# Attention and gated MLP on one core: z2 stores, maxima and sums on other queues, heads packed in pairs, refills by credit

## The chip, the cores and the metric

The kernel runs on one core of a Trainium2 chip, in float32. Its time is the device time of one execution in microseconds (us); the smaller the better. Every number of a profile is from one execution recorded by the hardware profiler.

## The reference

A sequence of 2048 rows of 576 is normalised once; attention and a gated MLP both read it, and the result is their product, gated, added to the input.

```python
xn = layernorm(x)
# attention: 32 heads of 18, a causal window of 256 keys
qkv = (xn @ wqkv).reshape(B, S, 3, 32, 18)
scores = einsum("bhqd,bhkd->bhqk", q, k) * 18 ** -0.5
mask = (q_row - k_row >= 0) & (q_row - k_row < 256)
s = softmax(where(mask, scores, -1e9)) @ v -> (B, S, 576) @ wo
# gated MLP
z = gelu(xn @ w_in)                       # 576 -> 4608
z1, z2 = z[..., :2304], layernorm(z[..., 2304:])
g = einsum("ts,bsf->btf", w_sp, z2) + b_sp   # mixes the 2048 rows
out = x + s * silu((z1 * g) @ w_out)
```

## The kernel before

Matrix products are made exact enough by splitting each operand into a rounded high part (ScalarE copies) and a low part (VectorE subtracts), and by three products of the parts. The program runs through six stages:

- **Start, Q and K** (0 to 176 us). Rows are normalised and transposed into `xt6`, Q and K come out transposed, and each strip is stored to `st_d` in DRAM: for Q and for K (first index), high and low parts of 18 rows each, by head. `load_wqkv` splits the weights; the low part is made by GpSimd (L259).
- **V** (to 208 us).
- **z2** (208 to 460 us): 6 x 16 steps of 14 matmuls (L686). ScalarE applies GELU into `zt` (L697), VectorE takes statistics, and two steps at a time are stored to `z2_d` by a DMA on ScalarE's queue (L700). Beside it GpSimd forms sums and differences of w_sp (`sp_combos`, L619 to L623), which SyncE loads (`a<-in_w_sp`) and stores (`sc_d<-a`). Six head loads and the first 42 steps of row maxima are put in too.
- **Attention with z1** (460 to 992 us): 16 units of four heads and half of the queries. A unit computes scores transposed (`tps`, L524), exponentials on ScalarE (`pt`, L528), causal masks on GpSimd (L531, L534) and the product with V (`ops`, L547), four steps later. Between these matmuls stand those of z1 (L445) and the maxima for the next unit.
- **Spatial mixing** (992 to 1716 us): w_sp @ z2 by seven products of blocks (a Strassen scheme), 168 steps of 18 matmuls (L960); each step needs a piece of w_sp and a piece of z2, which `z_unit` loads (`zr`) and forms. `pump` hands out these units.
- **Output** (1716 us to the end).

Row maxima: for unit u, `row_max` computes scores the other way round (`sp`, L395), a maximum per query on VectorE (L399), one transposition for all 32 maxima, and splits the negated maxima into two parts. `put_max` writes them by DMA on ScalarE's queue (L415) into rows 54 and 55 of the head's Q strip; there K has ones, so that the matmul itself subtracts the maximum. RMN is the number of steps of a unit, LEAD how many are done ahead of their unit.

A head lies in half of a slot (`att`, five slots of two heads): partitions 0 to 55 for even heads, 64 to 119 for odd ones. `load_head` fills it by four DMAs of SyncE (L362 to L365), of 36, 18, 20 and 36 partitions. Slots 3 and 4 are made and cleared where attention starts. LOAD_AT gives the items of a unit (32 or 40) ahead of which the loads of later heads stand.

When a unit's last block is out, `finish` gathers the softmax sums by a DMA on ScalarE's queue (`den<-ou`, L597); VectorE inverts them, SyncE stores them (`r_d`, L573) and reads them back, each head's over 32 partitions (`rp`, L577, 512 KB); VectorE multiplies, SyncE stores four strips (`o_d`, L588).

In the start the order of each engine's work comes from a scheduler; from z2 on it is the order in which the code writes it, for all five engines. Each engine waits in that order, and what stands behind a wait waits too. SyncE issues nearly all DMAs; a DMA that waits for its data holds up those behind it.

Of the kernel before, what the change touches and what calls it, by code (L numbers as in the profile page):

```python
# [62 lines left out]
def kernel(  # L63
# [20 lines left out]

    st_d = dram.tile([2, 38, H, S], F32, name="st_d")
    sc_d = dram.tile([4, 8, P, 1024], F32, name="sc_d")
# [21 lines left out]
    low = const.tile([64, 1], F32, name="low")  # L108
    dve.reduce_sum(low, ident[:64, :64].rearrange("p (a n b) -> p n a b", n=2, b=8)[:, 1], axis=mybir.AxisListType.XY)
    dve.tensor_scalar(low, low, -1.0, None, ALU.mult)  # L110
# [118 lines left out]
    with ExitStack() as early:  # L229
# [15 lines left out]
        with ExitStack() as ph:  # L245
# [7 lines left out]
            def load_wqkv(c):  # L253
                raw = pA.tile([P, 5, 192], F32, name="wraw", bufs=4)
                sp.dma_start(raw, wqkv[:, :, c * 192:(c + 1) * 192])
                to, c = (wq, c) if c < 6 else (wv, c - 6)
                cs = slice(c * 192, (c + 1) * 192)
                act.activation(to[0][:, :, cs], raw, AF.Copy)
                pool.tensor_tensor(to[1][:, :, cs], raw, f32(to[0][:, :, cs]), ALU.subtract)  # L259

# [39 lines left out]
            def qk_chunk(c):  # L300
                cs = slice(c * 512, (c + 1) * 512)
                for n, j in enumerate(range(9) if c < NC - 1 else (0, 4, 5, 1, 2, 3, 6, 7, 8)):
                    if n == NORM_AT and c + 1 < NC:
                        norm_chunk(c + 1)
                    js = slice(j * P, (j + 1) * P)
                    ps = mmp.tile([P, 512], F32, name="mm")
                    pl = list(passes(whq[:, :, js], wlq[:, :, js], cs))
                    for n, (w, r) in enumerate(pl):
                        pe.matmul(ps, w, r, start=n == 0, stop=n == len(pl) - 1)  # L309
                    hl = pA.tile([P, 2, 512], F32R, name="qkhl")  # L310
                    split(hl[:, 1], hl[:, 0], ps)
                    for n in range(2):
                        rows = st_d[n, 0:36, :, cs].rearrange("(c i) h s -> c i h s", c=2)[:, 2 * j:2 * j + 2]
                        sp.dma_start(rows.rearrange("c i h s -> (i h) c s"), f32(hl[64 * n:64 * n + 64]))
# [8 lines left out]
            for c in range(NC):  # L323
                if c + 1 < NC:
                    load_x(c + 1)
                qk_chunk(c)
                if c == 0:
                    for w in range(6, 9):
                        load_wqkv(w)
                    zero = pA.tile([H, 512], F32, name="zero", bufs=1)  # L330
                    pool.memset(zero, 0.0)
                    for k in range(NC):
                        for r in range(2):
                            sp.dma_start(st_d[0, 36 + r, :, k * 512:(k + 1) * 512], zero)
        aa = open_pool(early, "aa", bufs=2)
        slots = [aa.tile([P, SLOT], F32R, name=f"att{i}", bufs=1) for i in range(3)]

        with ExitStack() as ph:
# [17 lines left out]
            def load_head(u, j):  # L356
                g, half = UNITS[u]
                q0 = half * HS
                k0, kn = (0, HS) if half == 0 else (HS - 256, HS + 256)
                h, b = 4 * g + j, 64 * (j % 2)  # L360
# [23 lines left out]
            def row_max(u):  # L384
                g, half = UNITS[u]
                base = 0 if half == 0 else 6
                mx = aa.tile([P, 4, 2, 8], F32, name="mx")
                for j in range(4):
                    for i in range(8):
# [10 lines left out]
                                                 scalar=-3.0e38, op0=ALU.add, op1=ALU.max,  # L400
                                                 accum_out=mx[:, j, 0, i:i + 1])
# [4 lines left out]
                pe.transpose(pt[:64, :P], mx.rearrange("p a n b -> p (a n b)"), ident)  # L406
                spend(110)
# [100 lines left out]
            def scores(u, kb, qa, qz, j):  # L508
# [3 lines left out]
                if j == 0:  # L512
                    own = u == NU - 1 or len(seen) % NPT < 3
                    pts[u, kb] = ap_.tile([P, 4, 384], F32, name="pt", bufs=3) if own else ab.tile(
                        [P, 4, 384], F32, name="pt2", bufs=NPT - 3)
                    seen.append(u)
# [48 lines left out]
            def finish(u, ou):  # L565
# [30 lines left out]

                act.dma_start(den, ou[DH::32, :])  # L597
                after(6000 if u < NU - 2 else 2700, lambda: queue([invert]))
# [33 lines left out]
            with ExitStack() as gate:  # L632
# [35 lines left out]
                combos = sp_combos(gate)  # L668
                heads_at = {3 * NS + 4 * n: divmod(n, 4) for n in range(6)}
                stream = (step for u in range(NU) for step in row_max(u))  # L670
                for pc in range(6):
# [4 lines left out]
                    if pc == 1:  # L676
                        clear(0)
                        clear(1)
                    for s in range(NS):
                        ss = slice(s * P, (s + 1) * P)  # L680
# [11 lines left out]
                        if pc + 1 < 6 and s % 2 == 0:  # L692
                            next(nxt[2], None)
                        if s % 2 == 0:
                            zz = gz.tile([P, 2 * ZW], F32, name="zt", bufs=4)
                        zv = zz[:, s % 2 * ZW:s % 2 * ZW + ZW]
                        act.activation(zv, ps[:, :ZW], AF.Gelu_apprx_tanh)  # L697
# [9 lines left out]
                        if pc == 5:  # L707
                            dve.bn_aggr(mv2[:, s, :], st2[:, s].rearrange("p a b -> p (a b)"))
                for _ in combos:
                    pass  # L710
# [6 lines left out]
            with ExitStack() as heads:  # L717
                order.close()
                heads.enter_context(tc.manual_schedule(engines=HEADS))
                ab = open_pool(spare, "ab", side="right")  # L720
                for i in range(3, NSLOT):
                    slots.append(ab.tile([P, SLOT], F32R, name=f"att{i}", bufs=1))
                    clear(i)
                work = heads.enter_context(ExitStack())
# [109 lines left out]
    with ExitStack() as ph:  # L834
# [115 lines left out]
        for m, (g, n, s) in enumerate(order_sp):  # L950
# [22 lines left out]
            if s == 5:  # L973
                if g + 1 < NG:
                    units += [z_unit(wk, g + 1, k, b) for b in range(8)]
                elif n:
                    units += free_tile(n)
        while due or units or flying:
            now += 1
            for job in due.pop(now, ()):  # L980
                job()
            pump(1)

# [146 lines left out]
```

## Time and profile before

| what | before |
|---|---|
| median of 3 runs | 1982.95 us (1979.98 to 1985.52) |
| the profiled execution, its span | 1988.46 us, 1986.8 us |
| TensorE busy | 1926.1 us, 97% |
| VectorE, ScalarE, GpSimd busy | 1077.4, 890.8, 286.6 us |
| moved by DMA | 375.05 MB, mean 189 GB/s |
| DMA issues on SyncE's queue, on ScalarE's | 343.62 MB, 29.47 MB |

Busy is the time in which an engine works on something; the space between is idle, and the profile names what ended it. A wait counts only where the engine that sets the end waits, which here is TensorE in nearly all of the span. DMA share is a mean over 16 DMA engines.

### The profile page before, as it was taken

What the parts mean: (1) busy time and instruction counts of PE and PEld (TensorE: products, weight loads), DVE (VectorE), ACT (ScalarE), POOL (GpSimd) and SP (SyncE); (2) the same over time, 40 slices, a digit from 0 to 9 for tenths busy, and PEclk for the clock granted to TensorE, in tenths of its full rate; (3) what the DMA queues carried; (4) which work ended last, traced back from release to release, by engine and by line L of the source; (5) the groups of instructions that cost most, each with busy time, mean ns of one, the idle gap of its engine ahead of it and who ended that gap; (6) DMA issues with size and microseconds to landing.
All of it is one profiled execution on the core that took longest, in us unless ns stands there. A gap on an engine that the chain in (4) does not pass through costs nothing.

```text
span 1986.8 us, 30617 instructions
## 1 busy us (share of the span) xinstructions
PE 1926.1 (97%) x11096; PEld 1661.5 (84%) x11096; DVE 1077.4 (54%) x2286; ACT 890.8 (45%) x1647; POOL 286.6 (14%) x360
## 2 busy tenths in 40 slices
PE   6999999999999999999999999999999999999998
PEld 5889999997777777777688887888788888999998
DVE  6521233256666666666267768576866676523222
ACT  3222222215656656656575465645554445422121
POOL 5000363402222223333200000000000000000000
PEclk9999999999999999999999999999999999999999
DMA  7655798924454656464577578666775567844441
GB/s 221 178 145 146 248 302 265 300 92 126 134 154 135 162 137 161 128 157 115 171 264 240 174 261 271 214 211 217 237 247 182 180 219 247 293 138 141 141 143 56
DMA packets 218599, 375.05 MB, mean 189 GB/s; under 512 B 42960, under 2 KB 115536, under 8 KB 218320
## 3 DMA queue, kind: packets, MB, share of 16 engines
q1 hardware_dynamic: 197520, 343.62, 56.4%
q10 hardware_dynamic: 20928, 29.47, 4.1%
q8 instruction: 87, 1.43, 0.3%
q14 instruction: 64, 0.52, 0.1%
HBM read 259.92 MB, written 112.30 MB: 187 GB/s over the span
## 4 chain that ended last, share of the span: by engine, by line
PE 81%; DMA 11%; DVE 3%; ACT 1%; SPq 1%; issue 1%; POOL 1%; ACTq 0%; DVEq 0%; POOLq 0%
PE acc L960 32%; PE po L1057 12%; PE mm L445 10%; PE mm L686 5%; PE mm L309 5%; PE tps L524 4%; PE sp L395 4%; PE ops L547 3%; PE vps L463 3%; DMA sc_d<-a 3%; DMA att<-st_d 3%; PE wops L1027 2%; DMA a<-in_w_sp_dram 1%; DMA z1raw<-in_w_z_dram 1%; DMA att<-mhl 1%
## 5 line engine op out<-in xcount | busy, mean ns | idle before, releaser
L960 PE MATMUL acc<-sph,zh 128*128 128x512 f32 x1008 | 394.3, 391 | 8.2 <-DVE cb L914 8.2
L960 PE MATMUL acc<-spl,zh 128*128 128x512 f32 x1008 | 393.8, 391 | 0.0
L960 PE MATMUL acc<-sph,zl 128*128 128x512 f32 x1008 | 393.6, 390 | 0.0
L399 DVE CUSTOM_DVE_ANT_0 junk<-sp,band 128x384 bf16<-128x384 f32 (+1 forms) x512 | 272.7, 538 | 152.3 <-PE sp L395 148.1
L528 ACT ACTIVATE pt<-tps 128x384 f32<-128x384 f32 (+2 forms) x576 | 244.6, 438 | 144.7 <-PE tps L524 112.9
L445 PE MATMUL mm<-b,z1wh 128*128 128x512 f32 x648 | 250.7, 398 | 0.0
L213 DVE TENSOR_TENSOR spl<-spr,sph 128x1024 fp32r<-128x1024 f32 x166 | 203.1, 1224 | 62.9 <-ACT sph L213 61.7
L960 PEld LDWEIGHTS acc<-sph,zh 128*128 128x128 f32 x1008 | 190.2, 189 | 48.6 <-ACT zh L213 5.6
L960 PEld LDWEIGHTS acc<-sph,zl 128*128 128x128 f32 x1008 | 190.2, 189 | 40.0
L960 PEld LDWEIGHTS acc<-spl,zh 128*128 128x128 f32 x1008 | 190.3, 189 | 39.5
L524 PE MATMUL tps<-att 128*128 128x384 f32 (+1 forms) x576 | 189.6, 329 | 14.9 <-ACT pt L528 12.0
L686 PE MATMUL mm<-z2wh,b 128*128 128x384 f32 x720 | 194.3, 337 | 7.5 <-ACT zt L697 7.5
L213 ACT ACTIVATE zh<-b 128x384 fp32r<-128x384 f32 x144 | 75.8, 526 | 251.7 <-PE acc L960 251.6
L213 ACT ACTIVATE sph<-spr 128x1024 fp32r<-128x1024 f32 x166 | 174.2, 1049 | 21.5 <-DMA spr<-in_w_sp_dram 11.2
L395 PE MATMUL sp<-att 128*128 128x384 f32 (+1 forms) x512 | 171.3, 335 | 5.6 <-DMA att<-st_d 2.2
L1057 PE MATMUL po<-b,yh 128*128 128x288 f32 x896 | 155.6, 296 | 0.0
L213 DVE TENSOR_TENSOR zl<-b,zh 128x384 fp32r<-128x384 f32 x144 | 79.9, 555 | 124.2 <-ACT zh L213 124.2
L524 PEld LDWEIGHTS tps<-att 128*128 128x128 f32 x576 | 108.8, 189 | 41.7 <-ACT pt L528 25.0
L445 PE MATMUL mm<-b,z1wl 128*128 128x512 f32 x360 | 143.4, 398 | 0.0
L445 PEld LDWEIGHTS mm<-b,z1wh 128*128 128x128 f32 x648 | 121.6, 189 | 24.8 <-issue 6.4
L686 PEld LDWEIGHTS mm<-z2wh,b 128*128 128x128 f32 x720 | 131.5, 189 | 9.8 <-ACT zt L697 9.7
L686 PE MATMUL mm<-z2wl,b 128*128 128x384 f32 x400 | 134.3, 336 | 0.0
(154 smaller groups left out, 2793.0 us busy)
## 6 DMA issues: line engine op xcount, KB each, us to landing
spr<-sc_d SPq DMA_DIRECT2D x96, 512.0 KB
spr<-in_w_sp_dram SPq DMA_DIRECT2D x72, 512.0 KB
zr<-z_d SPq DMA_DIRECT2D x136, 192.0 KB
st_d<-qkhl SPq DMA_DIRECT2D x72, 256.0 KB
z_d<-zt ACTq DMA_DIRECT2D x48, 384.0 KB
z_d<-z1o SPq DMA_DIRECT2D x72, 256.0 KB
z1t<-z_d SPq DMA_DIRECT2D x72, 256.0 KB
y_d<-z1t SPq DMA_DIRECT2D x72, 256.0 KB
```

The lines of the kernel that those rows point to most:

```text
L213: job()
L309: pe.matmul(ps, w, r, start=n == 0, stop=n == len(pl) - 1)
L395: pe.matmul(ps[:, :w], q_of(u, j)[:, i * P:(i + 1) * P], k_of(u, j)[:, k0:k0 + w], start=True, stop=True)
L399: dve.tensor_tensor_reduce(out=junk[:, :w], in0=ps[:, :w], in1=band[:, m0:m0 + w], scale=1.0, scalar=-3.0e38, op0=ALU.add, op1=ALU.max, ac ...
L445: pe.matmul(ps, w, r, start=n == 0, stop=n == len(pl) - 1)
L463: pe.matmul(ps[:, i, :288], r, w[:, i * 288:(i + 1) * 288], start=n == 0, stop=n == len(pl) - 1)
L524: pe.matmul(ps[:, :m * P], k_of(u, j)[:, (kb - base) * P:(kb - base + 1) * P], q_of(u, j)[:, (a - lo) * P:(a - lo + m) * P], start=True, s ...
L528: act.activation(pt[:, j, d0:d0 + n * P], ps[:, (qa - a) * P:(qa - a + n) * P], AF.Exp, scale=scale)
L547: pe.matmul(o_ps[c][32 * j:32 * j + 32, (lo - 4 * c) * P:(hi - 4 * c + 1) * P], vgs[u][:, kb - k0, j * VW:j * VW + 32], pt[:, j, (lo - kb) ...
L686: pe.matmul(ps[:, :ZW], r, wt, start=n == 0, stop=n == len(pl) - 1)
L960: pe.matmul(acc[j], z[:, ps], w[:, cs], start=s == i == 0 and n in OPENS, stop=s == 7 and i == 2, skip_group_check=True)
L1057: pe.matmul(po[i][:, a, :288], y[:, i * P:(i + 1) * P], w[:, a * 288:(a + 1) * 288], start=f == 0 and m == 0, stop=f == NF - 1 and m == 2)
```

## The change

- z2 is stored one step at a time by SyncE, one step late, from five single `zt` tiles.
- The odd head of a slot moves from partitions 64 on to 54 on, so that both heads have their maxima in the slot's rows 54 and 55: `put_max` is one DMA for two heads, on GpSimd's queue. Even heads need their Q strip in another order, and `st_d` has its two zero rows behind the high rows. `load_head` reads some strips as two groups of 18 rows (`both`, a broadcast).
- The gathering of the sums goes to GpSimd's queue.
- Slots 3 and 4 are made and cleared within z2; ten heads are loaded there, and LOAD_AT shifts the later loads by an item or two.
- `row_max` has one more step, between the copy and the transposition; RMN, LEAD and HEAD follow.
- `pump` hands out loads by a credit (2 a step up to step 17, then 1.34), forms them at least two steps later, and the tiles for w_out are asked for one product later.
- The low parts of the weights of Q, K and V come from VectorE; the zero rows are stored a chunk later.

```diff
-RMN = 34
-LEAD = 8
+RMN = 35
+LEAD = 9
...
-LOAD_AT = (0, 2, 9, 16)
+LOAD_AT = (1, 9, 16, -1)
 TAIL = 66
-HEAD = 24
+HEAD = 12
...
-    def pump(n):
-
-        for _ in range(n):
-            need = units[0][2] if units else 9
-            if flying and (len(flying) == 4 or sum(f[2] for f in flying) + need > 5):
-                form, got, _ = flying.pop(0)
-                form(got)
-            if units:
-                load, form, need = units.pop(0)
-                flying.append((form, load(), need))
+    credit = 0.0
+
+    def pump(m):
+
+        nonlocal credit
+        credit = min(credit + (2 if m < 18 else 1.34), 2)
+        idle = 0
+        while units:
+            load, form, need = units[0]
+            if need > credit or sum(f[2] for f in flying) + need > ZRB or (need == 0 and idle == 2):
+                break
+            units.pop(0)
+            flying.append((form, load(), need, m))
+            credit -= need
+            idle += need == 0
+        for n in range(2):
+            if not flying or (n and flying[0][2] and m >= 24):
+                break
+            form, got, need, since = flying[0]
+            if m - since < (2 if need else 1):
+                break
+            flying.pop(0)
+            form(got)
...
-                pool.tensor_tensor(to[1][:, :, cs], raw, f32(to[0][:, :, cs]), ALU.subtract)
+                dve.tensor_tensor(to[1][:, :, cs], raw, f32(to[0][:, :, cs]), ALU.subtract)
...
-                sp.dma_start(q[b:b + 36, :], st_d[0, 0:36, h, q0:q0 + HS])
-                sp.dma_start(k[b:b + 18, :kn], st_d[1, 18:36, h, k0:k0 + kn])
-                sp.dma_start(q[b + 36:b + 56, :], st_d[0, 18:38, h, q0:q0 + HS])
-                sp.dma_start(k[b + 18:b + 54, :kn], st_d[1, 0:36, h, k0:k0 + kn])
+                qs, ks = st_d[0, :, h, q0:q0 + HS], st_d[1, :, h, k0:k0 + kn]
+                both = ks.rearrange("(c i) s -> c i s", c=2)[:, :18]
+                if j % 2 == 0:
+                    sp.dma_start(q[0:36, :], qs[20:38].unsqueeze(0).to_broadcast([2, 18, HS]))
+                    sp.dma_start(k[0:18, :kn], ks[20:38])
+                    sp.dma_start(q[36:56, :], qs[0:20])
+                    sp.dma_start(k[18:54, :kn], both)
+                else:
+                    sp.dma_start(q[54:74, :], qs[18:38])
+                    sp.dma_start(k[56:92, :kn], both)
+                    sp.dma_start(q[74:110, :], qs.rearrange("(c i) s -> c i s", c=2)[:, :18])
+                    sp.dma_start(k[92:110, :kn], ks[20:38])
...
                 dve.tensor_copy(mx[:, :, 1], mx[:, :, 0])
                 yield
+                yield
...
-                def put_max(j):
-                    b = 64 * (j % 2)
-                    act.dma_start(f32(q_of(u, j)[b + 54:b + 56, :]), f32(m[16 * j:16 * j + 16, :]))
-
-                for j in range(4):
-                    after(1200 + 900 * j, partial(put_max, j))
+                def put_max(n):
+                    t = slots[(2 * u + n) % NSLOT]
+                    pool.dma_start(f32(t[54:56, 0:2 * HS]), f32(m[32 * n:32 * n + 32, :]))
+
+                for n in range(2):
+                    after(1000 + 600 * n, partial(put_max, n))
...
-                act.dma_start(den, ou[DH::32, :])
+                pool.dma_start(den, ou[DH::32, :])
...
-                heads_at = {3 * NS + 4 * n: divmod(n, 4) for n in range(6)}
+                ab = open_pool(spare, "ab", side="right")
+                for i in range(3, NSLOT):
+                    slots.append(ab.tile([P, SLOT], F32R, name=f"att{i}", bufs=1))
+                heads_at = {3 * NS + 4 * n: divmod(n, 4) for n in range(10)}
+                z2_out = []
...
+                    if pc == 2:
+                        clear(3)
+                        clear(4)
...
-                        if s % 2 == 1:
-                            act.dma_start(z2_d[(s - 1) * P:(s + 1) * P, zc].rearrange("(a p) c -> p a c", p=P),
-                                          zz.rearrange("p (a c) -> p a c", a=2))
+                        z2_out.append((z2_d[s * P:(s + 1) * P, zc], zv))
+                        if len(z2_out) > 1:
+                            sp.dma_start(*z2_out.pop(0))
...
-                    heads_at = {LOAD_AT[i]: (u + 1 + i // 2, (2, 3, 0, 1)[i]) for i in range(4)}
+                    heads_at = {LOAD_AT[i] % len(items): (u + 1 + (i > 0), (3, 0, 1, 2)[i])
+                                for i in range(4) if u or i == 3}
...
-            pump(2 if m < 6 or (len(units) > 8 and m % 3 == 0) else 1)
+            pump(m)
...
-                elif n:
-                    units += free_tile(n)
+                elif n > 1:
+                    units += (free_tile(1) if n == 2 else []) + free_tile(n)
```

Three places where the order of instructions matters below. First, SyncE's order in the attention stage, around the V load and the sums of a unit; `att` is a slot, `z_d<-z1o` a store of z1, the last number of a row is the elements of a partition. Before:

```order
L500 DMA vg<-v_d 128x8x89
L362 DMA att_1208<-st_d 36x1024
L363 DMA att_1208<-st_d 18x1024
L364 DMA att_1208<-st_d 20x1024
L365 DMA att_1208<-st_d 36x1024
L377 DMA z_d<-z1o 128x512
L573 DMA r_d<-den 128x32
L577 DMA rp<-r_d 128x1x1024
```

Now:

```order
L523 DMA vg<-v_d 128x8x89
L384 DMA att_1208<-st_d 20x1024
L385 DMA att_1208<-st_d 36x1x1024
L386 DMA att_1208<-st_d 36x1x1024
L387 DMA att_1208<-st_d 18x1024
L399 DMA z_d<-z1o 128x512
L596 DMA r_d<-den 128x32
L600 DMA rp<-r_d 128x1x1024
```

Nothing moved here, but the strips of 36 partitions now have the form of the broadcast `rp`, with a step of one in the middle: their source has two groups.

Second, SyncE's order in z2, at two head loads (`sc_d<-a` stores a combination of w_sp, `z_d<-zt` a step of z2). Before:

```order
L362 DMA att_1208<-st_d 36x1024
L363 DMA att_1208<-st_d 18x1024
L364 DMA att_1208<-st_d 20x1024
L365 DMA att_1208<-st_d 36x1024
L627 DMA sc_d<-a_2857 128x512
L627 DMA sc_d<-a_2851 128x512
```

Now:

```order
L379 DMA att_1208<-st_d 36x1x1024
L380 DMA att_1208<-st_d 18x1024
L381 DMA att_1208<-st_d 20x1024
L382 DMA att_1208<-st_d 36x1x1024
L729 DMA z_d<-zt 128x384 x4
L384 DMA att_1208<-st_d 20x1024
L385 DMA att_1208<-st_d 36x1x1024
L386 DMA att_1208<-st_d 36x1x1024
L387 DMA att_1208<-st_d 18x1024
L650 DMA sc_d<-a_2913 128x512
```

The stores of z2, which stood on ScalarE's queue, are between and behind the head loads.

Third, the sums: on ScalarE before, between the eviction of a unit's output and the exponentials (`pt`) of the next:

```order
L528 ACTIVATE pt_4493<-tps 128x384 x4
L559 ACTIVATE ou<-ops 128x512
L597 DMA den<-ou 128x1x32
L528 ACTIVATE pt_4556<-tps 128x384 x3
L448 ACTIVATE z1o<-mm 128x512
```

Now on GpSimd, between the masks, as are the maxima:

```order
L557 AFFINE_SELECT pt<-pt 128x4x128
L438 DMA att_1208<-mhl 2x16x128
L438 DMA att_1209<-mhl 2x16x128
L554 AFFINE_SELECT pt<-pt 128x4x128
L554 AFFINE_SELECT pt_5371<-pt_5371 128x4x128
L554 AFFINE_SELECT pt_5417<-pt_5417 128x4x128
L557 AFFINE_SELECT pt_5417<-pt_5417 128x4x128
L620 DMA den<-ou 128x1x32
L554 AFFINE_SELECT pt<-pt 128x4x128
```

ScalarE no longer issues them; the masks that follow on GpSimd stand behind them.

More of the change, by code (lines that the diff above doesn't have):

```diff
@@ L83 @@
     dram = open_pool(ctx, "dram", space=DRAM)
-    st_d = dram.tile([2, 38, H, S], F32, name="st_d")
+    st_d = dram.tile([2, 40, H, S], F32, name="st_d")
     sc_d = dram.tile([4, 8, P, 1024], F32, name="sc_d")
@@ L108 @@
     low = const.tile([64, 1], F32, name="low")
-    dve.reduce_sum(low, ident[:64, :64].rearrange("p (a n b) -> p n a b", n=2, b=8)[:, 1], axis=mybir.AxisListType.XY)
+    dve.reduce_sum(low, ident[:64, :64].rearrange("p (a n b) -> p n a b", n=2, b=16)[:, 1], axis=mybir.AxisListType.XY)
     dve.tensor_scalar(low, low, -1.0, None, ALU.mult)
@@ L312, in qk_chunk @@
                     for n in range(2):
-                        rows = st_d[n, 0:36, :, cs].rearrange("(c i) h s -> c i h s", c=2)[:, 2 * j:2 * j + 2]
+                        rows = st_d[n, :, :, cs].rearrange("(c i) h s -> c i h s", c=2)[:, 2 * j:2 * j + 2]
                         sp.dma_start(rows.rearrange("c i h s -> (i h) c s"), f32(hl[64 * n:64 * n + 64]))
@@ L329 @@
                         load_wqkv(w)
+                if c == 1:
                     zero = pA.tile([H, 512], F32, name="zero", bufs=1)
@@ L333 @@
                         for r in range(2):
-                            sp.dma_start(st_d[0, 36 + r, :, k * 512:(k + 1) * 512], zero)
+                            sp.dma_start(st_d[0, 18 + r, :, k * 512:(k + 1) * 512], zero)
         aa = open_pool(early, "aa", bufs=2)
@@ L359, in load_head @@
                 k0, kn = (0, HS) if half == 0 else (HS - 256, HS + 256)
-                h, b = 4 * g + j, 64 * (j % 2)
+                h = 4 * g + j
                 q, k = f32(q_of(u, j)), f32(k_of(u, j))
-                sp.dma_start(q[b:b + 36, :], st_d[0, 0:36, h, q0:q0 + HS])
-                sp.dma_start(k[b:b + 18, :kn], st_d[1, 18:36, h, k0:k0 + kn])
-                sp.dma_start(q[b + 36:b + 56, :], st_d[0, 18:38, h, q0:q0 + HS])
-                sp.dma_start(k[b + 18:b + 54, :kn], st_d[1, 0:36, h, k0:k0 + kn])
+                qs, ks = st_d[0, :, h, q0:q0 + HS], st_d[1, :, h, k0:k0 + kn]
[10 more added lines that the diff above has]
+                    sp.dma_start(k[92:110, :kn], ks[20:38])
             waiting, seen, stored = [], [], set()
@@ L386, in row_max @@
                 base = 0 if half == 0 else 6
-                mx = aa.tile([P, 4, 2, 8], F32, name="mx")
+                mx = aa.tile([P, 2, 2, 2, 8], F32, name="mx")
                 for j in range(4):
@@ L400, in row_max @@
                                                  scalar=-3.0e38, op0=ALU.add, op1=ALU.max,
-                                                 accum_out=mx[:, j, 0, i:i + 1])
+                                                 accum_out=mx[:, j // 2, 0, j % 2, i:i + 1])
                         yield
@@ L404, in row_max @@
                 yield
+                yield
                 pt = sps.tile([P, 384], F32, name="sp")
-                pe.transpose(pt[:64, :P], mx.rearrange("p a n b -> p (a n b)"), ident)
+                pe.transpose(pt[:64, :P], mx.rearrange("p a n b i -> p (a n b i)"), ident)
                 spend(110)
@@ L513, in scores @@
                     own = u == NU - 1 or len(seen) % NPT < 3
-                    pts[u, kb] = ap_.tile([P, 4, 384], F32, name="pt", bufs=3) if own else ab.tile(
+                    pts[u, kb] = ap_.tile([P, 4, 384], F32, name="pt", bufs=3) if own else pb.tile(
                         [P, 4, 384], F32, name="pt2", bufs=NPT - 3)
@@ L693 @@
                             next(nxt[2], None)
[L694 to L696 removed]
+                        zv = gz.tile([P, ZW], F32, name="zt", bufs=5)
                         act.activation(zv, ps[:, :ZW], AF.Gelu_apprx_tanh)
                         dve.bn_stats(st2[:, s, pc, :], zv)
[L699 to L701 removed]
+                        z2_out.append((z2_d[s * P:(s + 1) * P, zc], zv))
+                        if len(z2_out) > 1:
+                            sp.dma_start(*z2_out.pop(0))
                         if pc == 5 and s == 6:
@@ L708 @@
                             dve.bn_aggr(mv2[:, s, :], st2[:, s].rearrange("p a b -> p (a b)"))
+                sp.dma_start(*z2_out.pop(0))
                 for _ in combos:
@@ L719 @@
                 heads.enter_context(tc.manual_schedule(engines=HEADS))
[L720 to L723, printed above, removed]
+                pb = open_pool(spare, "pb", side="right")
                 work = heads.enter_context(ExitStack())
@@ L981 @@
                 job()
-            pump(1)
+            pump(now)
     sets.close()
```

## The prediction

> **What bounds the kernel now.** I read the page's first table and its chain of waits, then the busy times by stage, then who waits for whom inside the stages, and last the DMA view of short stretches.
>
> ```profile
> PE 1926.1 (97%) x11096; PEld 1661.5 (84%) x11096; DVE 1077.4 (54%) x2286; ACT 890.8 (45%) x1647; POOL 286.6 (14%) x360
> ...
> 208.00:460.00 252.00, 244.55 (x1394) 241.70 (x1393) 96.56 (x213) 60.03 (x117) 88.78 (x66) 0.99 0.73 237
> 460.00:975.00 515.00, 493.62 (x3396) 381.16 (x3395) 325.69 (x1094) 310.92 (x732) 159.07 (x241) 1.00 0.55 146
> 992.00:1716.00 724.00, 715.83 (x3218) 595.94 (x3217) 500.51 (x698) 396.89 (x591) 0.00 (x0) 0.99 0.69 228
> ```
>
> The columns of a window are its length, busy PE, PEld, DVE, ACT and POOL, the granted clock, the DMA share and GB/s. TensorE is busy in 1926.1 of 1986.8 us. The 60.7 us without it are the most that hiding work could bring. In z2 (208 to 460) they are 7.45 us, in attention (460 to 975, 16 units, 515 / 16 = 32.2 us each) 21.4 us, in the spatial stage 8.2 us; the rest is at both ends. So a large gain isn't there, but a large loss can be, wherever another resource passes TensorE. The waits behind these 60 us, where the change touches them:
>
> ```profile
> PE mm L686 <- ACT zt L697: 7.5, 7, 2.2
> PE tps L524 <- ACT pt L528: 12.0, 12, 2.5
> PE tps L524 <- DMA att<-mhl: 2.8, 3, 1.1
> PE sp L395 <- POOL pt L534: 1.8, 1, 1.8
> PE acc L960 <- DVE cb L914: 8.2, 2, 5.2
> ```
>
> (What waits, for what: us in all, times, longest.) The second line is largely the sums' DMA on ScalarE:
>
> ```profile
> 557.98 0.60 ACT L559 ACTIVATE ou<-ops 128x512 f32<-128x512 f32 x1 [2.02 <-PE ops L547]
> 559.67 0.60 ACTq L597 DMA_DIRECT2D den<-ou  x1
> 560.32 0.60 ACT L448 ACTIVATE z1o<-mm 128x512 f32<-128x512 f32 x1 [1.74 <-PE mm L445]
> ...
> 561.35 0.44 PE L524 MATMUL tps<-att 128*128 128x384 f32 x1 [1.38 <-ACT pt L528]
> ```
>
> ScalarE issues it behind the eviction, no exponential runs for 1.74 us, and TensorE stands for 1.38 us. One such gap a unit.
>
> **The resource that the mean DMA share hides.** A mean of 0.55 over 16 DMA engines says nothing of one engine. Two stretches in which few transfers run tell more. From 513.6 to 516.3 us only the reciprocals' broadcast (rp, 512 KB) moves; from 522.8 on, head loads.
>
> ```profile
> q1 hardware_dynamic: 61, 0.25, 24.8%
> ...
> q1 hardware_dynamic: 347, 0.98, 67.9%
> ...
> 522.80:527.80 5.00, 5.00 (x48) 3.29 (x47) 3.00 (x11) 2.19 (x5) 1.37 (x3) 1.00 0.70 166
> ```
>
> The first row is the broadcast's DMA view: 61 rows of 4 KB, 24.8% of 16 engines, so 4 engines. Its source has four heads as outermost step, its target 128 partitions. One row takes 2.7 us x 16 x 0.248 / 61 = 0.176 us. The second is 6 us of head loads; they come to about 0.70 of 16 and stay under 12 / 16 = 0.75, though eight are in flight, of 36, 18, 20 and 36 rows. That fits 12, 9, 10 and 12 engines (the largest counts up to 16 that divide the rows), and always the same ones: eight loads on changing engines would fill all 16. Here a row takes 6 x 16 x 0.679 / 347 = 0.188 us over all packets, of which 101 are under 512 B; without these about 0.26 us.
>
> **The head loads, the main term.** Four DMAs bring a head, as before, with as many bytes. But two of the four now read one strip as two groups of 18 rows: the even heads' Q strip by a broadcast over a step of two, the others through `(c i)` with c = 2. The outermost step of the source is 2, that of the target 36 partitions. By the broadcast's pattern (4 against 128 gives 4 engines) this gives 2 engines with 18 rows each, where 36 rows had 12 engines with three.
>
> The page "DMA: Bandwidth & Descriptors" of the Trainium skill (section "Why a DMA increments its semaphore by 16 and not by 1") has this as a rule: the slowest dimension of each side, the largest count up to 16 that divides both, and on the hardware queues the lowest-numbered engines. The 24.8% agrees with it. By it the loads would run on two engines, always the first two, which is the forecast below.
>
> Engine time of the first two engines, in one unit, from the rows at 0.176 us for 4 KB (5 KB: 0.22):
> - half 0: 8 loads x 18 rows x 0.176 = 25.3 us (before: 8 x 3 x 0.176 = 4.2). Half 1, whose K rows have 5 KB: 4 x 18 x 0.176 + 4 x 18 x 0.22 = 28.5 us.
> - the loads of 18 and 20 rows, 2 rows an engine: 2.8 us, in half 1 3.2.
> - the rest, whose sizes the rows below give: rp 512 KB on 4 engines, 32 rows, 5.6; z1 stores 4.5 x 8 rows of 2 KB, 3.2; V 356 KB over 16 and w_z1 1.1 x 320 KB over 16, at 4 KB in 0.176, about 0.9 each; o_d 4 x 2 rows, 1.4. Sum 12.0, half 1 12.3.
>
> ```profile
> att<-st_d SPq DMA_DIRECT2D x84, 144.0 KB
> rp<-r_d SPq DMA_DIRECT2D x15, 512.0 KB
> ...
> att<-st_d SPq DMA_DIRECT2D x32, 180.0 KB
> z1raw<-in_w_z_dram SPq DMA_DIRECT2D x17, 320.0 KB
> ...
> o_d<-ou SPq DMA_DIRECT2D x60, 72.0 KB
> ...
> vg<-v_d SPq DMA_DIRECT2D x7, 356.0 KB
> ```
>
> That is 40.1 us a unit in half 0 and 44.0 in half 1, against 32.2 us of TensorE. It can't be hidden: the load of the second pair at a unit's last item is wanted by the maxima a fifth of a unit (6 us) later: nine of 35 steps are done ahead, and a third head begins at step 16, and every later DMA of SyncE, z1 stores too, queues on the same two engines. Units 1 to 13 bring 52 of the 64 heads (10 come in z2, one each in units 0 and 14): 5 x 40.1 + 8 x 44.0 = 552 us; units 0, 14 and 15 keep 32.2. Sum 649 us against 515: **+134 us**, if the two engines never idle. They do idle:
>
> ```profile
> SPq L577 <- DMA r_d<-den: 44.7, 13, 5.4
> ```
>
> SyncE holds rp until the reciprocals have landed, 3.4 us a time, and sends nothing meanwhile: 13 x 3.4 = 44 us more if the engines ran dry each time, +178. Part of it they spend on what is queued. I take **+150**. Bounds: rows a tenth faster than the broadcast's, which no view shows, and no idling: 552 x 0.9 + 97 = 594, +79; the head loads at the 0.26 us of the crowded ones (53.6 and 59.1 us a unit): +322. I stay near the broadcast, since it too runs on few engines.
>
> **z2 stores by SyncE.** 96 stores of 192 KB in place of 48 of 384 KB on ScalarE's queue; they stand in SyncE's order between the combinations' loads and stores, one step late.
>
> ```profile
> z_d<-zt ACTq DMA_DIRECT2D x48, 384.0 KB
> ...
> a<-in_w_sp_dram SPq DMA_DIRECT2D x64, 256.0 KB
> sc_d<-a SPq DMA_DIRECT2D x64, 256.0 KB
> ...
> SPq L500 <- DMA z_d<-zt: 46.9, 1, 46.9
> ```
>
> The last row says that SyncE had run ahead and waited 46.9 us at the stage's end; now each store holds it to ScalarE's pace (252 / 96 = 2.63 us a step), so the crowding at the start (DMA at 0.9 and over there on the page) spreads out and the 7.45 us of waits should go. Against it stand ten head loads, one in four steps. Four steps cost the first two engines 4 x (0.94 combinations + 0.53 stores + 0.14 weights) = 6.4 us, a head 2 x 3.2 + 4 x 0.176 = 7.0: 13.4 in 10.5 us. Ten times 2.9 is 29 us late; four free zt tiles hold 10.5 of it. Between -7.5 and +18 I take **+8**.
>
> **Off ScalarE's queue.** Sums and maxima (32 DMAs for two heads each, not 64) now stand on GpSimd behind the masks. That ends the gaps above, about 10 us, and most of the 2.8 for maxima, and slots 3 and 4 cleared in z2 end the 1.8 us at 473. In a stage set by DMA these are inside the +150, so nothing is taken off. No row shows a DMA on GpSimd; from nothing to 3 us of held masks (ScalarE's longest gap) each, it lies beside the same wait.
>
> **Start.** Nine subtractions go from GpSimd to VectorE, 1.15 us each by the 1024-wide row (1224 ns). GpSimd's held VectorE's small ones:
>
> ```profile
> 9.99 2.19 DVE L124 TENSOR_SCALAR tm<-tm 128x2 f32<-128x2 f32 x1
> ...
> 9.76 2.39 POOL L259 TENSOR_TENSOR wlq<-wraw,whq 128x960 fp32r<-128x960 f32 x1 [5.75 <-ACT whq L258]
> ```
>
> Three such holds of some 2 us go, two subtractions stand ahead of the second pair of rows instead: **-3** (between -6 and +3).
>
> **Spatial refills.** The same loads and forms, spread by a credit. The two gaps, 2.96 and 5.21 us, come where refills crowd ScalarE and VectorE. Between -8 and +6: **-4**.
>
> Sum: 1988.46 (profiled; span 1986.8) + 150 + 8 - 3 - 4 = 2139.5. The median lies 5.5 us under the profiled execution: **2134 us**.
>
> **Rivals.**
> - *As wide as before.* If the two-group form spreads over 12 engines, the rest counts: -10 sums, -2.8 maxima, -1.8 late slot, -7 z2, -3 start, some of 8 spatial: about 1960 us. For it: same bytes, same strips. Against it: the 24.8%. 0.07.
> - *Two engines, but changing ones.* Then no engine is overfull; a load lands 15 rows x 0.176 = 2.6 us later, which the 6 us just cover in most units: 0 to 2 us lost a unit against 20 gained, 1965 to 1990. Against it: 0.70, never over 0.75, with eight loads in flight. 0.06, half of it without a difference.
> - *GpSimd's queue bounds.* Masks stand behind a DMA that waits; PV has four steps of slack. It decides if one hold passes these 12 us; at 3 us a unit, 16 x 3 - 20 = +28, 2011 us. 0.04. "SBUF — State Buffer" of the Trainium skill (section "SBUF: two separate sides") says that VectorE can keep GpSimd from writing descriptors through the port they share; no run here shows a DMA on GpSimd yet, and VectorE's 63% in this stage leaves gaps.
>
> **Numbers.** The forecast has 0.83. Its own range is 2040 (1988.5 + 79 - 7.5 - 6 - 8 - 5.5: each term at its good end) to 2240 (the attention stage about halfway between +178 and +322, the rest as above). The other cases hold 0.17, so this is the range given. A measurement here tells about 0.3% (6 us). Faster 0.10, same 0.03, slower 0.87.
>
> **What will show it.** DMA share in attention falls while the stage grows to some 650 us, with long stretches near 0.125 (two of 16); TensorE waits on att<-st_d at scores and maxima, SyncE on landings; the unit is 40 us in half 0 and longer in half 1; ScalarE has no den gap. In z2 TensorE waits for zt from the first head load on. Wrong: head loads at 0.7 share, units of 32 us; or waits on GpSimd's masks.

## The result, and the profile after

The changed kernel takes 2180.83 us in the median (2176.11 to 2180.95), the kernel before in the same comparison 1984.24 us: a ratio of 1.0988 (95% interval 1.0964 to 1.1012), slower by a tenth. The profiled execution took 2176.11 us, its span is 2174.4 us.

The first table of the page, and busy times by stage, first of the changed kernel, then of the kernel before. The stages are cut where the last matmul of each ends: Q, K and V; z2 (of the changed kernel in two pieces, at 413 us); attention; spatial (in the kernel before it ends at 1690 us, not at 1716); output. The columns are those of the windows above.

```profile
PE 1965.6 (90%) x11096; PEld 1694.8 (78%) x11096; DVE 1078.5 (50%) x2295; ACT 889.7 (41%) x1647; POOL 294.0 (14%) x399
...
0.00:205.00 205.00, 188.88 (x1033) 164.00 (x1034) 78.36 (x167) 55.49 (x105) 22.22 (x45) 1.00 0.61 176
205.00:413.00 208.00, 189.16 (x1043) 187.24 (x1043) 60.69 (x93) 47.84 (x92) 72.98 (x55) 0.96 0.66 222
413.00:488.50 75.50, 65.36 (x346) 63.70 (x345) 38.87 (x125) 11.05 (x24) 16.99 (x14) 0.91 0.52 184
488.50:1192.20 703.70, 545.73 (x3481) 422.23 (x3480) 323.75 (x1093) 316.52 (x740) 181.81 (x286) 0.89 0.35 109
1192.20:1878.10 685.90, 685.74 (x3026) 567.69 (x3025) 482.78 (x674) 384.50 (x575) 0.00 (x0) 1.00 0.70 229
```

```profile
0.00:208.60 208.60, 190.94 (x1033) 165.99 (x1034) 76.29 (x158) 55.98 (x105) 38.13 (x52) 0.99 0.58 169
208.60:459.50 250.90, 243.45 (x1387) 240.69 (x1387) 96.56 (x213) 59.64 (x116) 88.78 (x66) 0.99 0.73 238
459.50:991.70 532.20, 510.82 (x3481) 394.36 (x3480) 327.73 (x1097) 315.94 (x740) 159.71 (x242) 1.00 0.54 145
991.70:1690.20 698.50, 690.33 (x3025) 570.44 (x3024) 482.53 (x674) 384.94 (x575) 0.00 (x0) 0.99 0.68 225
```

Attention grew by 171.5 us, while its DMA share fell from 0.54 to 0.35; z2 grew by 32.6; the start is 3.6 shorter and the spatial stage 12.6 shorter. TensorE's waits, longest first, show zt in z2, and in attention, ahead of all, the scores for the row maxima (sp), which wait for SyncE's DMAs ("issue": for nothing that the view can name); the wait for pt, 12.0 us before, is down to 8.9:

```profile
PE sp L417 <- DMA z_d<-z1o: 51.9, 6, 13.2
PE sp L417 <- issue: 33.3, 5, 9.9
PE mm L716 <- ACT zt L725: 27.5, 9, 5.8
PE sp L417 <- DMA o_d<-ou: 24.0, 3, 9.4
PE sp L417 <- DMA att<-st_d: 21.2, 3, 10.8
PE tps L547 <- DMA att<-mhl: 14.1, 9, 3.0
...
PE tps L547 <- ACT pt L551: 8.9, 5, 3.2
```

One unit at SyncE, and the DMA view of 668 to 673 us, where little but the loads issued in these rows is in flight:

```profile
663.75 0.63 SPq L384 DMA_DIRECT2D att<-st_d  x1
664.43 0.61 SPq L385 DMA_DIRECT2D att<-st_d  x1
665.09 0.60 SPq L386 DMA_DIRECT2D att<-st_d  x1
665.74 0.61 SPq L387 DMA_DIRECT2D att<-st_d  x1
666.45 0.35 SPq L596 DMA_DIRECT2D r_d<-den  x1
675.40 0.58 SPq L600 DMA_DIRECT2D rp<-r_d  x1
```

```profile
DMA packets 87, 0.26 MB, mean 52 GB/s; under 512 B 25, under 2 KB 25, under 8 KB 87
...
q1 hardware_dynamic: 87, 0.26, 13.1%
```

13.1% of 16 engines is 2.1 engines, with the two loads of two groups (L385, L386) under way together: both are on the same two engines. The 62 rows of 4 KB in it took 5 x 16 x 0.131 / 62 = 0.169 us each. SyncE's rp waits from 666.8 to 675.4 us for the reciprocals (`r_d`, 16 KB), which were issued behind these rows; in the median they land 8.1 us after their issue, in e1 below, without loads of two groups, 3.7.

The trace also holds the landing events of each DMA. Two-group loads have 3, plain loads of 18, 20 and 36 rows have 10, 11 and 13, and rp has 5: one more than the engines that the shares gave (2 here, 4 for rp). From issue to the last of these events the two-group loads take 8 to 12 us in the median, where the 36-row loads of before took 4.4 to 5.4. These events also tell what the scores waited for: each of the 14 waits of sp of over 3 us, whatever the view names, ends 0.1 to 0.4 us behind the landing of L387, the last load of an odd head.

### The profile page after: what moved, and what is told of

Same layout as the page of the kernel before. It is cut to its first block, busy times and chain, and to the rows that moved or that the text cites. A ratio compares the mean times of both kernels' runs of the same rounds, so it can differ in the third digit from the quotient of the medians.

```text
span 2174.4 us, 30802 instructions
## 1 busy us (share of the span) xinstructions
PE 1965.6 (90%) x11096; PEld 1694.8 (78%) x11096; DVE 1078.5 (50%) x2295; ACT 889.7 (41%) x1647; POOL 294.0 (14%) x399
## 4 chain that ended last, share of the span: by engine, by line
PE 71%; DMA 24%; SPq 2%; issue 1%; DVE 1%; ACT 1%; DVEq 0%; ACTq 0%
PE acc L987 31%; PE po L1084 11%; DMA att<-st_d 7%; PE mm L716 7%; PE mm L468 6%; PE mm L322 5%; DMA r_d<-den 4%; DMA z_d<-z1o 3%; PE wops L1054 3%; PE vps L486 3%; PE sp L417 3%; DMA rp<-r_d 3%; PE tps L547 2%; DMA sc_d<-a 2%; DMA z1raw<-in_w_z_dram 1%; DMA o_d<-ou 1%
## 5 line engine op out<-in xcount | busy, mean ns | idle before, releaser
L417 PE MATMUL sp<-att 128*128 128x384 f32 (+1 forms) x512 | 184.3, 361 | 136.4 <-DMA z_d<-z1o 51.9
L468 PE MATMUL mm<-b,z1wh 128*128 128x512 f32 x648 | 263.3, 419 | 0.0
L716 PE MATMUL mm<-z2wh,b 128*128 128x384 f32 x720 | 202.4, 350 | 27.5 <-ACT zt L725 27.5
L417 PEld LDWEIGHTS sp<-att 128*128 128x128 f32 x512 | 105.4, 206 | 149.3 <-issue 136.2
L547 PE MATMUL tps<-att 128*128 128x384 f32 (+1 forms) x576 | 198.1, 344 | 23.0 <-DMA att<-mhl 14.1
L716 PEld LDWEIGHTS mm<-z2wh,b 128*128 128x128 f32 x720 | 137.8, 198 | 30.4 <-ACT zt L725 30.4
L547 PEld LDWEIGHTS tps<-att 128*128 128x128 f32 x576 | 116.8, 203 | 49.7 <-ACT pt L551 21.7
L468 PEld LDWEIGHTS mm<-b,z1wh 128*128 128x128 f32 x648 | 129.9, 201 | 27.5 <-issue 6.8
L468 PE MATMUL mm<-b,z1wl 128*128 128x512 f32 x360 | 150.0, 417 | 0.0
```

The source lines that it names most:

```text
L417: pe.matmul(ps[:, :w], q_of(u, j)[:, i * P:(i + 1) * P], k_of(u, j)[:, k0:k0 + w], start=True, stop=True)
L547: pe.matmul(ps[:, :m * P], k_of(u, j)[:, (kb - base) * P:(kb - base + 1) * P], q_of(u, j)[:, (a - lo) * P:(a - lo + m) * P], start=True, s ...
L716: pe.matmul(ps[:, :ZW], r, wt, start=n == 0, stop=n == len(pl) - 1)
```

## The experiments

Lengths of the stages in us, between the ends of their last matmuls:

| stage | before | changed | e1 | e2 | e5 | e6 | e9 | e11 |
|---|---|---|---|---|---|---|---|---|
| start, Q, K, V | 208.7 | 205.1 | 206.2 | 206.8 | 205.7 | 207.2 | 207.6 | 205.5 |
| z2 | 250.9 | 283.6 | 248.1 | 270.7 | 250.1 | 261.8 | 250.5 | 283.8 |
| attention | 532.2 | 703.7 | 529.4 | 729.3 | 524.5 | 592.9 | 534.3 | 675.5 |
| spatial | 698.6 | 685.9 | 685.9 | 694.7 | 685.9 | 685.9 | 685.9 | 685.9 |
| whole span | 1986.8 | 2174.4 | 1965.4 | 2199.4 | 1962.1 | 2043.4 | 1973.7 | 2146.5 |

In the diffs, rows 0 to 17 of a strip are the low part and 20 to 37 the high part; the zero rows, 18 and 19, stand between them (behind the low part, not behind the high one, as the section on the change has it).

**e1: the form undone.**

```diff
-                    sp.dma_start(q[0:36, :], qs[20:38].unsqueeze(0).to_broadcast([2, 18, HS]))
+                    sp.dma_start(q[0:18, :], qs[20:38])
+                    sp.dma_start(q[18:36, :], qs[20:38])
...
-                    sp.dma_start(k[18:54, :kn], both)
+                    sp.dma_start(k[18:36, :kn], ks[0:18])
+                    sp.dma_start(k[36:54, :kn], ks[20:38])
...
```

> The changed kernel in which each head load of two groups of 18 rows is written as two loads of 18 rows; the same bytes, six DMAs a head in place of four, all else as changed. Theory (the two-group form runs on two DMA engines, and that alone makes the loss): the attention stage goes from 703.7 us back under the 532 us of the kernel before, to 510 to 525 us, since the sums and maxima are off ScalarE's queue; z2 from 283.5 us to 243 to 251 us; the granted clock in attention from 0.89 to 1.00; in all 1940 to 1975 us. Rival (the stores of z2 and the sums on new queues, or SyncE's order, cost the time): attention stays above 620 us, in all over 2100 us. Rival (SyncE's issue of more DMAs a head bounds): between, 2000 to 2100 us, with TensorE waiting on att behind SyncE's issues and not on landings.

Measured 1966.88 us, ratio 0.9898 (0.9856 to 0.9940): faster than before by one per cent. z2 came out as expected, and the granted clock in attention nearly (0.98). The whole loss of the changed kernel, 214 us, hangs on the form of these loads, and the other queues and orders cost nothing beside it. Attention is only 2.8 us under before, above the 510 to 525 expected; TensorE's waits there:

```profile
PE tps L550 <- DMA att<-mhl: 7.6, 5, 2.8
...
PE sp L420 <- DMA z_d<-z1o: 5.1, 2, 2.8
PE sp L420 <- DMA att<-st_d: 2.2, 1, 2.2
PE tps L550 <- ACT pt L554: 1.9, 2, 1.6
```

The 12 us for exponentials (pt) of before are 1.9, but 7.6 (2.8 before) go to maxima and 5.1 to SyncE's DMAs.

**e2: the form alone, in the kernel before.**

```diff
-    st_d = dram.tile([2, 38, H, S], F32, name="st_d")
+    st_d = dram.tile([2, 40, H, S], F32, name="st_d")
...
-                sp.dma_start(q[b:b + 36, :], st_d[0, 0:36, h, q0:q0 + HS])
+                sp.dma_start(q[b:b + 36, :], qs.rearrange("(c i) s -> c i s", c=2)[:, :18])
...
-                sp.dma_start(k[b + 18:b + 54, :kn], st_d[1, 0:36, h, k0:k0 + kn])
+                sp.dma_start(k[b + 18:b + 54, :kn], ks.rearrange("(c i) s -> c i s", c=2)[:, :18])
```

> The kernel before with one thing of the change: the strips lie 20 rows apart in st_d, and the two 36-row loads of each head are read as two groups of 18 rows. Four DMAs a head as before; z2 stores, sums, maxima, order and refills as before. Theory: the form alone brings the loss of the attention stage, 532 us to 680 to 720 us, with a share of DMA of about 0.13 in its quiet stretches; z2 with six heads in place of ten and its stores on ScalarE's queue loses 0 to 15 us; in all 2130 to 2190 us. Rival (the form hurts only together with the new order and queues): under 2050 us. Rival (the loss is the queue order): 1980 to 1990 us.

Measured 2200.50 us, ratio 1.1109 (1.1045 to 1.1173): the form alone brings the loss, and more of it than I expected. Attention is 25.6 us longer than in the changed kernel. Here the maxima and the sums are still on ScalarE's queue; a group of ScalarE's, with its idle time and what ended it:

```profile
L530 ACT ACTIVATE pt<-tps 128x384 f32<-128x384 f32 (+2 forms) x576 | 245.0, 438 | 316.5 <-PE tps L526 244.8 <-DMA att<-st_d 46.2 <-DMA rp<-r_d 6.8
```

```profile
PE tps L526 <- ACT pt L530: 61.3, 14, 7.4
```

The maxima go into a slot that is still being filled; the DMA waits on ScalarE's queue, the exponentials wait behind it (46.2 us), and TensorE for them (61.3 us, 8.9 in the changed kernel). This is not what makes most of the 25.6 us. 18.4 of them lie ahead of the first rp, which comes 78.6 us into the stage (556.1 - 477.5), in the changed kernel 60.2 us (548.7 - 488.5): there this kernel loads four heads that the changed kernel has loaded in z2. Over the twelve units behind it, with four head loads each in both kernels, it takes 46.2 us a unit against 45.3, 10.5 us in all. What ScalarE's queue costs has to be looked for in these, and no run takes it by itself. z2 loses 19.8 us with six heads, 3.3 a head.

**e3: fewer DMAs a head.** K's strips next to each other in st_d, so that its 36 rows are one plain load; five DMAs a head, not six.

> As the split version, but the K strips lie next to each other in st_d, so that K's 36 rows are one plain load again (12 engines) and a head has five DMAs. Theory: within 5 us of the split version, 1940 to 1975 us, since neither keeps any engine full. Rival (SyncE's issues count): 5 to 20 us faster than the split version.

Measured 1963.91 us, ratio 0.9892 (0.9849 to 0.9935), against e1's 0.9898: the same. SyncE's issues don't count here.

**e4: sums on ScalarE's queue, in e1.**

```diff
-                pool.dma_start(den, ou[DH::32, :])
+                act.dma_start(den, ou[DH::32, :])
```

> The split version with the gathering of the sums back on ScalarE's queue. Theory (one gap of ScalarE a unit, about 10 us in all, was the price there): 6 to 12 us slower than the split version, TensorE again waiting for pt some 12 times. Rival (that gap is covered, or GpSimd's queue holds as much): within 4 us.

Measured 1970.93 us, ratio 0.9925 (0.9897 to 0.9952); its interval overlaps e1's, and attention takes 529.5 us as in e1. TensorE waits for pt 10 times again, but only 4.4 us in all:

```profile
PE tps L550 <- ACT pt L554: 4.4, 10, 1.0
```

The rival held, at its edge (the medians are 4.05 us apart): the sums' DMA is not worth 10 us here. What else made the 12.0 us of before is not shown. The maxima's place alone does not: with them on ScalarE's queue and the sums off it (e7) the wait is 1.9 us, as in e1.

**e5: the same four DMAs, nested the other way.**

```diff
-                    sp.dma_start(q[0:36, :], qs[20:38].unsqueeze(0).to_broadcast([2, 18, HS]))
+                    sp.dma_start(q[0:36, :], qs[20:38].unsqueeze(1).to_broadcast([18, 2, HS]))
...
-                both = ks.rearrange("(c i) s -> c i s", c=2)[:, :18]
-                    sp.dma_start(k[18:54, :kn], both)
+                    sp.dma_start(k[0:36, :kn], ks.rearrange("(c i) s -> i c s", c=2)[:18])
...
```

> The changed kernel with the same four DMAs a head, the same strips and bytes, and only the nesting turned: the loads of 36 rows take row i of both groups one after the other (18 outer, 2 inner) in place of group after group (2 outer, 18 inner). Q and K rows are turned in the same way, so that the products are the same. Theory (the count of DMA engines divides the outermost steps of both sides): these loads land on 9 engines, attention at 525 to 535 us, z2 at 246 to 250 us, in all 1955 to 1975 us, like the split version. Rival (a broadcast, or any load that is not one contiguous block of rows, goes to few engines): over 2100 us, as in the changed kernel.

Measured 1966.87 us, ratio 0.9916 (0.9884 to 0.9949). The strips, bytes and count of DMAs are those of the changed kernel, a broadcast is still a broadcast, and the loss is gone. These loads have 10 landing events, as plain loads of 18 rows have, and land in 4.2 to 5.2 us. So it is the outermost step, 2 or 18, that sets the engines. The Trainium skill says so in "DMA: Bandwidth & Descriptors", section "Rules for kernel authors": an outermost dimension of a size c below 16, such as a leading broadcast of c copies, confines the whole DMA to at most c engines. The trace agrees, for the broadcast and for the `(c i)` source alike: 3 landing events with 2 outermost, 10 with 18.

**e6: half the dose.** K plain as in e3, Q still in two groups, four DMAs a head.

> The changed kernel with half of the dose: K's strips lie next to each other in st_d and are read by plain loads of 36 rows, Q's 36 rows are still read as two groups of 18. Theory (the sum of the first two engines' time decides, 0.176 us a row of 4 KB): 12.7 + 2.1 + 2.8 + 12.0 = 29.6 us a unit in half 0, 12.7 + 2.6 + 3.2 + 12.3 = 30.8 in half 1, and 2 to 3 us of idling as the changed kernel showed (its units took 42.3 and 46.7 us where the same sums gave 40.1 and 44.0): 32 and 33.5 us against 33.1 in the split version. Nearly all is covered: attention 528 to 550 us, in all 1965 to 1995 us. Rival (every two-group load has its price): half of the loss remains, attention about 615 us, in all about 2070 us.

Measured 2049.84 us, ratio 1.0339 (1.0301 to 1.0376). Neither held: attention at 592.9 us is 63.5 over e1, more than the theory's 21 at most, less than the rival's half (87). The sums left the two engines below TensorE's pace, and yet a unit took 4.5 us more: from rp to rp, over the twelve units with four head loads each, it is 37.1 us (521.1 to 966.3), in e1 32.6 (502.2 to 893.3). The sums for these units are (4.5 x 29.6 + 7.5 x 30.8) / 12 = 30.4 us.

**e7: maxima on ScalarE's queue, in e1.**

```diff
-                    pool.dma_start(f32(t[54:56, 0:2 * HS]), f32(m[32 * n:32 * n + 32, :]))
+                    act.dma_start(f32(t[54:56, 0:2 * HS]), f32(m[32 * n:32 * n + 32, :]))
```

> The split version with the maxima back on ScalarE's queue, still one DMA for two heads; the sums stay on GpSimd's. Theory (in the split version TensorE waits 7.6 us for maxima, where before it waited 2.8, since GpSimd's DMAs land later, 3.5 us in the median and up to 7.9): those waits fall to about 3 us and ScalarE's gaps (pt) take back 2 to 4 us: 1960 to 1970 us, the same within 5 us. Rival (ScalarE's queue pays for each DMA as the sums did before): 6 to 12 us slower.

Measured 1961.32 us, ratio 0.9889 (0.9859 to 0.9919): the same as e1 within the intervals; attention 525.6 us, the wait for maxima 4.6 in place of 7.6. The time is as expected, but ScalarE's gaps did not come back (TensorE waits 1.9 us for pt, as in e1), and no rule follows from 4 us.

**e8: z2 stored from ScalarE's queue, in e1**, each step right behind its GELU.

> The split version with each step of z2 stored from ScalarE's queue, right behind its GELU, not by SyncE a step later. Theory (SyncE's place spreads the crowding): z2 250 to 256 us in place of 248.1, TensorE waiting 7 to 13 us for zt in place of 5.7; in all 2 to 8 us slower. Rival (SyncE's stores are held by other DMAs, so that ScalarE's queue is as good): within 2 us, or faster.

Measured 1979.88 us, ratio 0.9981 (0.9962 to 1.0001): slower than e1 by 13 us. z2 takes 260.5 us, more than either expected, and TensorE waits twice as long for zt as in e1 (5.7):

```profile
PE mm L719 <- ACT zt L728: 11.5, 10, 3.9
```

96 issues on ScalarE, without the lag of one step, cost more than SyncE's 96. But the kernel before had 48 on ScalarE and took 250.9 us, 2.8 more than e1, and these 2.8 us hold the other changes in z2 too; what the move to SyncE is worth there is not shown by itself.

**e9: the refill rule alone, in the kernel before** (`pump`, its two calls and the request for w_out's tiles, as in the diff above).

> The kernel before with the new refill rule of the spatial stage alone (credit, forming two steps later, the tiles for w_out one product later). Theory (the 12.7 us by which the spatial stage is shorter in the changed kernel are the refills'): the stage goes from 698.6 to 686 to 688 us, without TensorE's gaps on cb; all other stages unchanged; in all 8 to 13 us under the kernel before of this comparison. Rival (a part of it comes from GpSimd's or SyncE's state at the stage's start, or from the clock after a stage of waits): 692 us or more in the stage.

Measured 1974.29 us against 1982.22, ratio 0.9959 (0.9941 to 0.9977): 7.9 us, just short of the 8 to 13. The spatial stage takes 685.9 us, without a gap:

```profile
980.00:1680.00 700.00, 699.85 (x3099) 579.59 (x3099) 486.54 (x680) 388.42 (x581) 0.00 (x0) 1.00 0.69 227
```

**e10: e5 with e7's queue.**

> The pairs-inside version with the maxima on ScalarE's queue. Theory: each alone was within noise of the split version (1966.9, 1961.3 us), together 1957 to 1967 us, about 1% under the kernel before. Rival: the two do not add, or ScalarE's gaps show: 1965 to 1972 us.

Measured 1964.58 us, ratio 0.9906 (0.9883 to 0.9929): as good as e1, e3, e5 and e7, and no better. Undoing the form in any of these ways leaves a kernel about 1% faster than before; which of them is used can't be told from the times. About 8 of the 18 us are the refill rule's (e9).

**e11: no hold for the reciprocals, in the changed kernel.**

```diff
-                    sp.dma_start(rp, r_d[u].unsqueeze(1).to_broadcast([4, 32, HS]))
+                    sp.dma_start(rp, r_d[max(u - 1, 0)].unsqueeze(1).to_broadcast([4, 32, HS]))
```

> The changed kernel, but the broadcast of the reciprocals (rp) reads the unit before in r_d, which landed long ago; same form, bytes and place in SyncE's order. The output is normalised by the wrong sums; SyncE no longer holds its queue for the landing of r_d (97.3 us in the changed kernel, 16 times). Theory (the two engines ran dry in that hold, and the units' time above the sum of their rows, 2.2 us in half 0 and 2.7 in half 1, is this): attention falls from 703.7 us by 25 to 45 us, to 660 to 680 us, units of 40 to 44 us. Rival (the two engines are fed throughout, the excess is slower rows): within 8 us of 703.7.

Measured 2148.61 us, ratio 1.0834 (1.0810 to 1.0858). Attention falls by 28.2 to 675.5 us, inside the 25 to 45. The issues of rp (count, times in ns, first and last start), of the changed kernel and then of this one:

```profile
L600 SPq DMA_DIRECT2D rp<-r_d x14: 577/582/596, 548.7 to 1125.5; - x14
```

```profile
L600 SPq DMA_DIRECT2D rp<-r_d x14: 574/578/733, 549.1 to 1098.5; - x14
```

Over the first twelve of the 13 stretches between them, to 1092.1 and 1062.5 us, four heads are loaded in each, 18 of half 0 and 30 of half 1 in all (in the last only two). These units take 45.3 us with the hold and 42.8 without; the sums of the prediction give (4.5 x 40.1 + 7.5 x 44.0) / 12 = 42.5. With the hold gone the two engines are the pace, to within a per cent.

**e12: the same, in e6.**

> The half dose (Q in two groups, K plain) with the same rp from the unit before; the output is normalised by the wrong sums. There SyncE held 60.3 us for r_d, and attention took 592.9 us where 528 to 550 were expected. Theory A (the hold and the dry engines made the difference): attention 540 to 560 us. Theory B (rows of 4 KB take 0.21 us, not 0.176, when other DMAs run beside them, so the first two engines need some 34 to 36 us a unit): attention stays above 575 us.

The profiled execution took 7610.50 us, for a reason that I don't know, and nothing is read from it; the three others took 2036 to 2041, 2036.62 in the median (2038.85 with the first), ratio 1.0276 (1.0246 to 1.0305). So there is no stage to read, but the whole is only 13 us under e6, where theory A wanted 33 to 53. The hold is not e6's main excess. Theory B fits better: over e6's attention stage rows of 4 KB took 0.192 us with three or four packets in flight and 0.206 to 0.219 with more (means of 1,059 and 6,569 packets); in the changed kernel the first figure is 0.177 (2,239 packets). At 0.21 e6's sums are 35.3 and 36.8 us a unit, (4.5 x 35.3 + 7.5 x 36.8) / 12 = 36.2 over the twelve; with 1.1 for the hold (13 / 12) that is 37.3, and 37.1 was measured. But this is a fit, and not proof: rows with five or more packets in flight took 0.21 us in the changed kernel's attention too (some 5,800 of them), and there the sums at 0.176 came out. Why a row's price held there and not here stays open.

## Why the prediction was right, and where its terms were off

It said 2134 us, 2040 to 2240, from two overfull engines. The measured 2180.83 is inside, 46.8 above the forecast. That owes something to the width of the main term's bounds, +79 to +322, since two of the smaller terms left theirs. By terms, against the profiled execution of before:

| term | predicted | bounds | measured |
|---|---|---|---|
| head loads in attention | +150 | +79 to +322 | +171.5 |
| z2 | +8 | -7.5 to +18 | +32.6 |
| start | -3 | -6 to +3 | -3.6 |
| spatial refills | -4 | -8 to +6 | -12.6 |
| profile to median | -5.5 | | +4.7 |

- **Two engines, always the same** was right, and shown: by the 13.1% with two such loads in flight, by e1, e2 and e5. The signs named for it are there: stretches at 0.13 (for 35% of the attention stage just two DMA packets are in flight, in e1 for 2%), maxima that wait for SyncE's loads, zt in z2. The rivals "as wide as before" and "changing engines" fall with it; the price named for the first, about 1960 us, is near what the kernel takes when its loads are wide (e1 and e5, 1967). "GpSimd's queue bounds" falls too: in e1, with the masks behind these DMAs, TensorE waits for no mask.
- **The attention term** lay between its +134 (never idle) and +178 (dry at each hold), but nearer the upper end than I took it. The rows' price was right for this kernel: e11's units are the sums. The step that was short is "part of it they spend on what is queued": the sum has 16 us for SyncE's hold (150 - 134), and taking the hold away gave 28.2. SyncE held rp 97.3 us in all, not 44, since the reciprocals that it waits for now land later (8.1 us after their issue). Without the hold attention is still 143.3 us over before, 9 more than +134; these 9 are not explained. SyncE's waits for the reciprocals:

```profile
SPq L600 <- DMA r_d<-den: 97.3, 16, 9.1
```

- **z2 was outside its bounds.** TensorE stands 28.98 us there (208 - 189.16 and 75.5 - 65.36). That this is the 10 x 2.9 = 29 us of the lateness is chance: without loads of two groups (e1) it still stands 248.0 - 240.89 = 7.1 us. So the loads stop it for some 22 us, where the prediction's own figures give 29 - 10.5 = 18.5. Six heads cost 3.3 us each in e2, ten 3.6 each here against e1. Two steps failed. That "the 7.45 us of waits should go" did not hold: 7.1 are left in e1. And TensorE's busy time rose by 11.1 us (254.5 against 243.45) for the same matmuls, at a granted clock of 0.96 and 0.91; I had no term for that. 28.98 - 7.45 + 11.1 = 32.6. The row of e1's z2:

```profile
206.00:454.00 248.00, 240.89 (x1388) 239.31 (x1387) 101.85 (x216) 58.96 (x116) 90.21 (x69) 1.00 0.74 242
```

- **The spatial term was outside too**, for the same reason with the other sign. Its gaps, 8.2 us, went as sized at the far end; with them went 4.6 us of slower matmuls behind them (690.33 to 685.74 us busy). e9 shows that the refill rule does it alone.
- **The gains from the queues were overrated.** The "about 10 us" for the gathering on ScalarE's queue, which was not in the forecast's sum, is at most 4 (e4). Of z2's 7.45, which was in it, nearly nothing went. In attention one wait takes the place of another.

## What to carry to other kernels

Look at the outermost step of both sides of every DMA: with the same strips and bytes, 2 outside and 18 inside ran on two engines and cost 214 us, 18 outside and 2 inside cost nothing that can be measured. A mean DMA share hides this; a stretch in which few transfers run shows it as a plateau at 2/16 or 4/16. And price a row in such a stretch only for a kernel whose engines are as empty: in crowded stretches it was a fifth dearer, and the sums of the half dose (e6) came out a fifth short.

## What the hardware showed that was not expected

A stop of TensorE costs more than the stop. The matmuls behind the longest gap of z2, in the changed kernel (groups in order of time; the gap in brackets):

```profile
383.63 1.01 PE L716 MATMUL mm<-z2wh,b 128*128 128x384 f32 x2 [5.85 <-ACT zt L725]
384.43 0.52 PE L716 MATMUL mm<-z2wl,b 128*128 128x384 f32 x1
...
387.95 0.52 PE L716 MATMUL mm<-z2wl,b 128*128 128x384 f32 x1
388.27 0.60 PE L716 MATMUL mm<-z2wh,b 128*128 128x384 f32 x2
388.71 0.34 PE L716 MATMUL mm<-z2wl,b 128*128 128x384 f32 x1
```

One starts every 0.32 us in place of every 0.175, for 4.6 us: some 2 us on top of 5.85. A gap of 2.96 us, in the spatial stage of before, had the same tail:

```profile
1222.00:1228.00 6.00, 3.34 (x8) 0.66 0.47 170
1228.00:1236.00 8.00, 8.00 (x31) 0.83 0.67 199
```

(Length, busy TensorE, granted clock, DMA share, GB/s.) "TensorE: Matmul & The Clock Gate" of the Trainium skill, section "Part 1: The HAM clock gate", has the clock fall to half after an idle window of about 3.4 us; the traces agree in kind, and here 2.96 us were enough. Whether the slow matmuls of attention (busy time up by 34.9 us) cost anything is another matter: there the DMA engines set the pace, and e11's units leave little room for it.

A small one: rp, the broadcast that was to tell how such loads run, is itself on four engines and takes 8.4 to 9.2 us from issue to landing (medians) in all kernels where I looked.
